# Which engine masks the diagonal blocks of the second batch, in decay attention followed by a max-MoE on one core

## The chip, the cores and the metric

The kernel runs on one core of one Trainium2 chip. The metric is the device time in microseconds (us) of one execution. The engines work side by side, each through its own instructions in order: TensorE (PE in the rows) multiplies matrices into PSUM, VectorE (DVE) and ScalarE (ACT) work element by element, GpSimd (POOL) reduces over partitions and casts, SyncE (SP) issues the transfers. An engine waits at the first instruction whose input is not there, and all that is queued behind it waits too.

## What is computed

```python
# q, k, v: 8 batches x 8 heads x 576 x 64; f: 8 x 8 x 576
scores = scale * q @ k.T + cum[:, None] - cum[None, :]    # cum: cumulated log of f
scores = where(key later than query, -1e9, scores)
attn = exp(scores - max) / (sum + 1e-9)
x = (attn @ v) laid out as 4608 tokens x 512
h = max(x @ w1, x @ w2, x @ w3)                            # 512 -> 768
out = h @ w_out                                            # 768 -> 512
```

Scores whose key is later than the query are masked. With keys on the partitions and queries along the row, this is a triangle in each 128 x 128 block on the diagonal, five per head (the fifth is 64 wide).

## The kernel before

**Heads.** The 64 heads are done one after another, eight to a batch. Each head is cut into unit 2, the first 256 queries (one PSUM bank, s2), and unit 1, the other 320 (three banks, s10 to s12). A unit's scores come in two passes on TensorE: pass A multiplies queries and keys (L647, two matmuls for unit 2, five for unit 1); then the diagonal blocks are masked; ScalarE and VectorE take the maximum over key blocks (L714, L702, L704, L707), GpSimd over the partitions (L717), and casts it into a row of the query tile (L720); pass B (L647 again) subtracts it by a further accumulation in the same bank. ScalarE takes the exponential (L735), VectorE or ScalarE and GpSimd sum it for the denominators where TensorE does not (L744 to L759).

**Masks.** Heads below MASKS are masked by TensorE, one small bf16 matmul of an identity with the mask per diagonal block (L663), accumulated in the bank between pass A and pass B. The others are masked by VectorE, which adds the mask to the bank in place: `cover` (L676, two blocks at a time; both units) and `cover_last` (L681, the 64 wide block; unit 1 alone).

**Pairs.** Two heads form a pair. TensorE multiplies the probabilities with the values (L803), and in the first two batches also sums them (L822). Of the sums, ScalarE takes a copy (L828); a transfer brings it into the tile sc, VectorE adds a small number and inverts (L898, L899), a second transfer writes to DRAM (rdram), a third reads it back widened (r_r), and VectorE multiplies the pair's values by it (L909). The result is one 128-row slice of x: ScalarE and VectorE split it into two parts (L914 xh, L916 xl).

**MoE.** For each batch, gemm1 (L940) runs over the four pairs of a batch and three matrices, three matmuls per pair and matrix (xh, xl, xh); gemm2 (L969) follows with three matmuls per block of 128 hidden columns. All weights are loaded, split (L511 to L523) and kept by then.

**Order.** All steps are handed to a planner (`Plan.add`) with engine, a cost and a due number, in units of a head. `Plan.emit` places, engine by engine, the due steps whose inputs it counts as there, and the kernel then issues them in that order. The constants that the change touches are offsets of these due numbers (WR and DPW for weights, LO, FO, VO1 and XO1 for the first two batches' sums, values and splits, lag for the MoE of the first batch), a preference for matmuls that follow one of like kind (LIKE), and the distance by which the load of a weight waits for an earlier one (PD).

Of the kernel before, what the change touches and what calls it, by code (L numbers as in the profile page):

```python
# [48 lines left out]
class Plan:  # L49
# [10 lines left out]
    ROOM = {"PE": (0.93, 0), "ACT": (1.0, -20.0), "DVE": (1.0, 0.0), "POOL": (1.0, 400.0), "SP": (1.0, 0)}  # L60
    LATE = 350.0
    MORE = (0.0, 100.0, 125.0, 0.0, 250.0)
    LIKE, HOLD = 4.0, 0.4

    def __init__(self):
        self.steps, self.wrote, self.read, self.parts = [], {}, {}, {}
# [1 line left out]
    def add(self, eng, cost, fn, r=(), w=(), prio=0.0, xfer=0.0, rows=128, short=0.0, light=False):  # L68
        i = len(self.steps)
        r, w = ([p for k in keys for p in self.parts.get(k, [k])] for keys in (r, w))  # L70
        deps = set()
        for k in r:
            if k in self.wrote:
                deps.add(self.wrote[k])
        for k in w:
            if k in self.wrote:
                deps.add(self.wrote[k])
            deps.update(self.read.pop(k, ()))
        for k in w:
            self.wrote[k] = i  # L80
        for k in r:
            if k not in w:
                self.read.setdefault(k, set()).add(i)
        deps.discard(i)
        self.steps.append((eng, cost, fn, deps, prio, xfer, rows, short, light))
# [86 lines left out]
def act_cost(cols):  # L172
    return 0.833 * cols + 60
# [7 lines left out]
def kernel(  # L181
# [33 lines left out]
    def sb(name, shape, dt=F32):  # L215
        return sbuf.tile(shape, dt, tag=name, name=name)
# [56 lines left out]
    NU = 5  # L273
    NB32 = 1

    MASKS, WIDE, COPIES = 16, 16, 64
    UT = [sb(f"u{i}", [P, S]) for i in range(KT)]

    XB = [sb(t, [P, 2, S2], F32R) for t in (f"u{KT}", "r")]
# [23 lines left out]
    def retire(old, new):  # L303
        gone = set()
        for key in [p for k in old for p in plan.parts.get(k, [k])]:
            gone |= plan.read.get(key, set()) | ({plan.wrote[key]} if key in plan.wrote else set())
        for key in [p for k in new for p in plan.parts.get(k, [k])]:
            plan.read.setdefault(key, set()).update(gone)
# [41 lines left out]
    def unit_w(i, fb):  # L350
        return lazy(f"w{3 * fb + i}", [P, 2, KT, P])

    def unit_o(fb):
        return lazy(f"w{3 * FT + fb}", [P, 2, DM])
# [12 lines left out]
    def dma(dst, src, r=(), w=(), prio=0.0, bytes_=300000):  # L367
        add("SP", 475 if bytes_ > 200000 else 640, lambda: nc.sync.dma_start(out=dst, in_=src), r, w, prio, bytes_ / 360)
# [118 lines left out]
    def load_weights(step, prio):  # L487

        if step < 3 * FT:
            i, fb = step % 3, step // 3  # L490
            src, n, m = (w1, w2, w3)[i].rearrange("(c p) f -> p c f", p=P), KT, P
            c0, c1 = fb * P, fb * P + P
            half = lambda t: unit_w(i, fb)[:, t]
        else:
            fb = step - 3 * FT
            src, n, m = w_out[fb * P:(fb + 1) * P, :].rearrange("(c p) e -> p c e", p=P), 1, DM
            c0, c1 = 0, DM
            half = lambda t: unit_o(fb)[:, t:t + 1]
        PD = 8
        raw, x = RAW[step], XW[step % len(XW)]  # L500
        key, kx, kh, kl = f"w{step}", f"x{step % len(XW)}", f"wh{step}", f"wl{step}"
        cols = lambda t: t.rearrange("p (c x) -> p c x", c=n)
        after = [f"wh{step - PD}"] if step >= PD else []
        if src.dtype == F32:
            dma(cols(raw.bitcast(F32)[:, 0:512]), src[:, :, c0:c1], w=[key], prio=DPW)
            add("DVE", 602, lambda: nc.vector.tensor_copy(x, raw[:, 0:512]), [key], [kx], prio)
        else:

            add("SP", 560, lambda: nc.sync.dma_start(out=cols(raw), in_=src.bitcast(I32)[:, :, 2 * c0:2 * c1]),  # L511
                after, [key], DPW + 0.01 * step, 524288 / 360)
            pair = raw.rearrange("p (x t) -> p x t", t=2)
            top, low = pair[:, :, 1], pair[:, :, 0]
            add("ACT", act_cost(512) + 40, lambda: nc.scalar.activation(
                top.bitcast(F32), top.bitcast(F32), AF.Prelu, scale=2.0 ** -112, alpha=2.0 ** 32), [key], [key], prio)
            add("DVE", 335, lambda: nc.vector.tensor_scalar(
                x, low, 29, None, op0=ALU.logical_shift_right), [key], [kx], prio)
            add("DVE", 602, lambda: nc.vector.scalar_tensor_tensor(
                x, top, 3, x, op0=ALU.logical_shift_left, op1=ALU.bitwise_or), [key, kx], [kx], prio)  # L520
        val = cols(x.bitcast(F32))
        add("ACT", act_cost(512) + 40, lambda: nc.scalar.activation(half(0), val, AF.Copy), [kx], [kh, key], prio)
        add("DVE", 602, lambda: nc.vector.tensor_tensor(half(1), val, half(0).bitcast(F32), op=ALU.subtract),  # L523
            [kx, kh], [kl], prio)
# [458 lines left out]
    def moe(b, prio):  # L983
        base = b * S
        if b % 2 == 0:
            chunks = [
                (0, S2, [main + (0, 0, S2)], [main + (0, 0), main + (128, 128)]),
                (S2, S1, [main + (0, 0, S2), midb + (S2, 0, 64)], [main + (0, S2), main + (128, S2 + 128)]),
            ]
        else:  # L990
            chunks = [
                (0, S1, [main + (64, 0, S2), midb + (0, 64, 64)],
                 [midb + (0, -64), main + (0, 64), main + (128, 192)]),
                (S1, S2, [main + (0, 0, S2)], [main + (0, S1), main + (128, S1 + 128)]),
            ]
        tot = sum(FT * 36 * mm_cost(c[1], P) + len(c[3]) * 18 * mm_cost(512, P) for c in chunks)
        done = 0.0
        for c0, cn, parts, outs in chunks:
            for fb in range(FT):
                gemm1(b, c0, cn, fb, parts, prio(done / tot))  # L1000
                done += 36 * mm_cost(cn, P)
            for hh, hl, kh, kl, col, row in outs:
                gemm2(hh, hl, kh, kl, col, base + row, prio(done / tot))
                done += 18 * mm_cost(512, P)


    LEAD, MLAG, WP, WR = 2.1, -0.1, 0.7, 0.65
    DP = -10.9
    DPW = 8.0
    ROWS = -4.0  # L1010
    warm_up()
    decay()
    QP = -0.3
    UO = 1
    LO = -2.55
    UP, VO, FO, XO = 0.4, 1.8, 0.5, -3.0
    HP, VP = -1.8, 0.6
    SP_ = 1.25
    HC, VO1, XO1, QP1, CB = -0.4, -1.2, -3.3, 0.7, -0.15
    order = (1, 2) if UO else (2, 1)  # L1020
    for n in range(H):
        load_raw(n, n - 8.9)
# [4 lines left out]
    for unit, up in ((2, 0.0), (1, 0.7)):  # L1027
        for n in range(H):
# [6 lines left out]
            if n % 4 == 3:  # L1035
                finish_group(n // 4, unit, p + LO)
    for n in range(H):
        retire([f"raw{n}/0", f"raw{n}/1"], [f"w{NW - H + n}"])
    for wstep in range(4 * FT):
        load_weights(wstep, WP + WR * wstep)  # L1040
# [11 lines left out]
    retire(["vn1"], [f"hdh{x}" for x in fbs])  # L1052
    for t in ("hmh", "hml"):
        retire([c + t for c in ("mx", "pf")] + [f"mx{t}a"], [f"{t}{x}" for x in fbs])
    lag = 0.15
    moe(0, lambda x: H + lag + H * x)
    retire([f"rs{g}{u}" for g in range(2) for u in (1, 2)], ["ph1"])
    retire([f"xa{x}" for x in range(KT)], ["pl1"])
# [63 lines left out]
```

## Time and profile before

| | |
|---|---|
| time, median of 3 runs | 905.31 us (905.06 to 907.84) |
| the profiled execution's own time | 907.01 us |
| its span in the trace | 905.2 us |
| mean granted clock of TensorE | 0.998 |
| TensorE busy, of the span | 895.2 us |
| VectorE, GpSimd, ScalarE busy | 630.1, 423.0, 387.8 us |
| matmul records in the trace | 6682 |

The profiled execution took 907.01 us, of which the span holds 905.2; 1.8 us lie around it. It is 1.7 us above the median. A busy TensorE means that matmuls were in its pipeline; how fast they follow one another is read from the distance of their starts, since their durations overlap.

### The profile page before, as it was taken

What the parts mean: (1) busy time and instruction counts of PE and PEld (TensorE: products, weight loads), DVE (VectorE), ACT (ScalarE), POOL (GpSimd) and SP (SyncE); (2) the same over time, 40 slices, a digit from 0 to 9 for tenths busy, and PEclk for the clock granted to TensorE, in tenths of its full rate; (3) what the DMA queues carried; (4) which work ended last, traced back from release to release, by engine and by line L of the source; (5) the groups of instructions that cost most, each with busy time, mean ns of one, the idle gap of its engine ahead of it and who ended that gap; (6) DMA issues with size and microseconds to landing.
All of it is one profiled execution on the core that took longest, in us unless ns stands there. A gap on an engine that the chain in (4) does not pass through costs nothing.

```text
span 905.2 us, 18386 instructions
## 1 busy us (share of the span) xinstructions
PE 895.2 (99%) x6682; PEld 809.6 (89%) x6682; DVE 630.1 (70%) x1427; ACT 387.8 (43%) x900; POOL 423.0 (47%) x380
## 2 busy tenths in 40 slices
PE   8999999999999999999999999999999999999998
PEld 6899988889989998988989898988989898998998
DVE  6989854577859796786858787796957678672211
ACT  6887633354334443443434443444334443342111
POOL 5443132336455645545555765556455464650000
PEclk9999999999999999999999999999999999999999
DMA  7995144555454456446445554546434454401000
GB/s 195 300 227 174 36 135 121 143 129 160 97 150 128 113 136 148 120 93 182 94 111 143 135 132 119 146 95 175 97 101 131 117 158 117 105 15 37 1 35 24
DMA packets 96867, 110.32 MB, mean 122 GB/s; under 512 B 51861, under 2 KB 64405, under 8 KB 96778
## 3 DMA queue, kind: packets, MB, share of 16 engines
q1 hardware_dynamic: 96778, 109.15, 46.4%
q8 instruction: 53, 0.87, 0.4%
q14 instruction: 36, 0.29, 0.1%
HBM read 49.56 MB, written 9.86 MB: 66 GB/s over the span
## 4 chain that ended last, share of the span: by engine, by line
PE 92%; DVE 3%; DMA 2%; ACT 1%; issue 1%; SPq 0%; ACTq 0%; DVEq 0%
PE mp L940 48%; PE mp L969 17%; PE s L647 13%; PE t L803 9%; PE t L772 1%; DMA w<-in_moe_w_dram 1%; DMA ks_r<-hl 1%; PE t L822 1%; PE mp L473 1%; DVE va_s L751 0%; DVE hl L536 0%; PE s L453 0%; PE mp L647 0%; PE s L663 0%; DVE hdl_r L954 0%
## 5 line engine op out<-in xcount | busy, mean ns | idle before, releaser
L940 PE MATMUL mp<-xh_r,w_r 128*128 128x320 f32 (+1 forms) x2160 | 462.3, 298 | 1.5 <-DVE tm L949 1.4
L940 PEld LDWEIGHTS mp<-xh_r,w_r 128*128 128x128 f32 x2160 | 355.8, 188 | 11.0 <-issue 4.7
L940 PE MATMUL mp<-xl_r,w_r 128*128 128x320 f32 (+1 forms) x1080 | 319.5, 296 | 0.0
L759 POOL PARTITION_ALL_REDUCE z<-va_s x96 | 193.8, 2018 | 160.6 <-DVE va_s L751 61.8
L717 POOL PARTITION_ALL_REDUCE gm<-mx x131 | 154.7, 1181 | 200.9 <-DVE mx L704 80.2
L940 PEld LDWEIGHTS mp<-xl_r,w_r 128*128 128x128 f32 x1080 | 203.3, 188 | 0.5
L949 DVE TENSOR_TENSOR tm<-mp,tm 128x256 f32<-128x256 f32 (+1 forms) x192 | 86.4, 450 | 86.0 <-PE mp L940 80.1
L647 PEld LDWEIGHTS s<-qs_r,ks_r 128*128 128x128 f32 (+1 forms) x784 | 116.2, 181 | 19.0 <-issue 14.0
L647 PE MATMUL s<-qs_r,ks_r 128*128 128x320 f32 (+4 forms) x784 | 132.2, 284 | 0.5 <-DMA ks_r<-hl 0.5
L969 PE MATMUL mp<-w_r,hmh_r 128*128 128x512 f32 (+1 forms) x396 | 122.7, 392 | 0.0
L707 DVE TENSOR_TENSOR mx<-mx,s 128x320 f32<-128x320 f32 (+3 forms) x248 | 92.2, 372 | 19.7 <-PE s L647 6.2
L969 PEld LDWEIGHTS mp<-w_r,hmh_r 128*128 128x128 f32 x396 | 70.1, 188 | 13.6 <-issue 1.8
L952 ACT ACTIVATE hmh_r<-tm 128x256 fp32r<-128x256 f32 x96 | 39.9, 416 | 96.4 <-DVE tm L949 95.8
L969 PE MATMUL mp<-w_r,hml_r 128*128 128x512 f32 (+1 forms) x198 | 76.9, 388 | 0.0
L947 ACT ACTIVATE tm<-mp 128x256 f32<-128x256 f32 (+1 forms) x96 | 39.6, 412 | 80.4 <-PE mp L940 76.0
L536 DVE STREAM_TRANSPOSE hl<-hl 128x576 f32<-128x576 f32 x56 | 68.4, 1242 | 4.8 <-DMA hl<-in_k_dram 4.8
L735 ACT ACTIVATE pf<-s 128x512 f32<-128x512 f32 (+4 forms) x107 | 49.0, 504 | 41.8 <-PE s L647 41.0
L954 DVE TENSOR_TENSOR hml_r<-tm,hmh_r 128x256 fp32r<-128x256 f32 x96 | 47.8, 498 | 17.6 <-ACT hmh_r L952 17.1
L720 POOL CAST qs_r<-gm 1x256 fp32r<-1x256 f32 (+1 forms) x112 | 56.4, 504 | 7.1
L676 DVE TENSOR_TENSOR s<-s,mask 128x256 f32<-128x256 f32 x96 | 40.6, 423 | 23.6 <-PE s L647 23.3
L735 ACT ACTIVATE ph_f<-s 128x384 f32<-128x384 f32 x80 | 36.0, 505 | 46.7 <-PE s L647 46.6
L714 ACT ACTIVATE mx<-s 128x320 f32<-128x320 f32 x56 | 24.4, 436 | 49.5 <-DVE s L681 42.1
(211 smaller groups left out, 1250.4 us busy)
## 6 DMA issues: line engine op xcount, KB each, us to landing
qs_r<-hl SPq DMA_DIRECT2D x168, 144.0 KB
ks_r<-hl SPq DMA_DIRECT2D x168, 144.0 KB
w<-in_moe_w_dram SPq DMA_DIRECT2D x18, 512.0 KB
out_dram<-o_r SPq DMA_DIRECT2D x35, 256.0 KB
hl<-in_q_dram SPq DMA_DIRECT2D x14, 576.0 KB
hl<-in_k_dram SPq DMA_DIRECT2D x14, 576.0 KB
r_r<-rdram SPq DMA_DIRECT2D x56, 144.0 KB
vn<-in_v_dram SPq DMA_DIRECT2D x30, 128.0 KB
```

Source lines behind the costliest of these rows:

```text
L536: add("DVE", 1085, lambda e=e, tt=tt, xs=xs: nc.vector.transpose(tt[:, e], xs[:, e]), [key + "0"], [key + "1"], prio)
L647: nc.tensor.matmul(bank[bk][0:l.shape[-1], col:col + w], l, rhs(qa, w), start=start and bk not in begun, stop=stop, skip_group_check=True)
L707: nc.vector.tensor_tensor(mt[:, a:a + w], mt[:, a:a + w], bank[bk][:, col:col + w], op=ALU.max)
L717: add("POOL", 450 + 2.6 * nq, lambda: nc.gpsimd.partition_all_reduce(gm, mt, P, bass.bass_isa.ReduceOp.max), [km, km + "a"], [kg], prio - CB)
L720: add("POOL", 130 + 0.9 * nq, lambda: nc.gpsimd.tensor_copy(QS(s)[96:97, 1, q0:q0 + nq], gm[96:97, :]), [kg], [kx], prio - CB)
L735: add("ACT", act_cost(w), lambda bk=bk, w=w, col=col: nc.scalar.activation(px()[:, col:col + w], bank[bk][:, 0:w], AF.Exp, scale=sc), [kb[ ...
L759: add("POOL", 520 + 5.1 * nq, lambda: nc.gpsimd.partition_all_reduce(Z[:, q0:q0 + nq], blocks_sum()[:, q0:q0 + nq], P, bass.bass_isa.Reduc ...
L803: nc.tensor.matmul(t[D * j:D * j + D, qa:qa + w], vn[:, j, c, 0:D], prs[j][0]()[:, col:col + w], start=x == 0, stop=True, skip_group_check ...
L940: nc.tensor.matmul(m, unit_w(i, fb)[:, w, kt, :], xx, start=kt == 0 and x == 0, stop=kt == KT - 1 and x == 2,)
L949: add("DVE", dve_cost(cn), lambda m=m: nc.vector.tensor_tensor(t, m, t, op=ALU.max), [km, kt_], [kt_], prio)
L954: add("DVE", dve_cost(w), lambda hh=hh, hl=hl, a=a, d=d, w=w: nc.vector.tensor_tensor(hl()[:, fb, d:d + w], t[:, a:a + w], hh()[:, fb, d:d ...
L969: nc.tensor.matmul(mp[:, 0:cn], l[:, fb, cs], unit_o(fb)[:, r, ds], start=fb == 0 and x == 0, stop=fb == FT - 1 and x == 2,)
```

## The change

MASKS goes from 16 to 8: the eight heads of the second batch (8 to 15) get L676 twice and L681 once on VectorE in place of five L663 matmuls on TensorE. Nine constants of the planner change with it.

```diff
-    LIKE, HOLD = 4.0, 0.4
+    LIKE, HOLD = 4.25, 0.4
...
-    MASKS, WIDE, COPIES = 16, 16, 64
+    MASKS, WIDE, COPIES = 8, 16, 64
...
-        PD = 8
+        PD = 7
...
-    LEAD, MLAG, WP, WR = 2.1, -0.1, 0.7, 0.65
+    LEAD, MLAG, WP, WR = 2.1, -0.1, 0.7, 0.8
     DP = -10.9
-    DPW = 8.0
+    DPW = 7.0
...
-    LO = -2.55
-    UP, VO, FO, XO = 0.4, 1.8, 0.5, -3.0
+    LO = -2.85
+    UP, VO, FO, XO = 0.4, 1.8, 1.0, -3.0
...
-    HC, VO1, XO1, QP1, CB = -0.4, -1.2, -3.3, 0.7, -0.15
+    HC, VO1, XO1, QP1, CB = -0.4, -0.95, -3.5, 0.7, -0.15
...
-    lag = 0.15
+    lag = 0.3
```

The order on TensorE is the same up to the first pass A of head 8 (66 us in the trace of before), and from some 225 us on nearly so: what differs there is a few exchanges between 706 and 816 us. Between 66 and 225 us the steps of the second batch and those of the first batch's MoE are interleaved anew, on all engines. There are three places that matter below.

**Place 1, TensorE, where the MoE of the second batch begins.** In the names, s10 to s12 are unit 1's banks, s2 is unit 2's, qs1/ks1 the odd heads' queries and keys, mp0 to mp2 gemm banks, w0 to w2 the first blocks of w1, w2, w3. Before, from the last matmul of pass A of head 17, unit 1:

```order
L647 MATMUL s12_127<-qs1_r_622,ks1_r_782 128x320
L969 MATMUL mp0_130<-w20_r_1246,hmh_r_953 128x512 x2
L969 MATMUL mp0_130<-w20_r_1246,hml_r_962 128x512
L969 MATMUL mp0_130<-w21_r_1294,hmh_r_953 128x512 x2
L969 MATMUL mp0_130<-w21_r_1294,hml_r_962 128x512
L969 MATMUL mp0_130<-w22_r_1310,hmh_r_953 128x512 x2
L969 MATMUL mp0_130<-w22_r_1310,hml_r_962 128x512
L969 MATMUL mp0_130<-w23_r_1363,hmh_r_953 128x512 x2
L969 MATMUL mp0_130<-w23_r_1363,hml_r_962 128x512
L647 MATMUL s2_128<-qs1_r_622,ks1_r_782 128x256
L647 MATMUL s2_128<-qs1_r_622,ks1_r_782 128x128
L940 MATMUL mp1_131<-xh_r_964,w0_r_505 128x320
```

After, from the same matmul:

```order
L647 MATMUL s12_127<-qs1_r_621,ks1_r_780 128x320
L940 MATMUL mp0_130<-xh_r_956,w2_r_594 128x320
L940 MATMUL mp0_130<-xl_r_1174,w2_r_594 128x320
L940 MATMUL mp0_130<-xh_r_956,w2_r_594 128x320
L647 MATMUL s2_128<-qs1_r_621,ks1_r_780 128x256
L647 MATMUL s2_128<-qs1_r_621,ks1_r_780 128x128
L940 MATMUL mp1_131<-xh_r_956,w0_r_504 128x320
L940 MATMUL mp1_131<-xl_r_1174,w0_r_504 128x320
L940 MATMUL mp1_131<-xh_r_956,w0_r_504 128x320
L940 MATMUL mp2_132<-xh_r_956,w1_r_532 128x320
L940 MATMUL mp2_132<-xl_r_1174,w1_r_532 128x320
L940 MATMUL mp2_132<-xh_r_956,w1_r_532 128x320
```

Before, the rest of the first batch's gemm2 stood behind this pass A, then pass B of unit 2, then 27 matmuls of gemm1 on the first three pairs, then pass A of head 18's unit 2 with pass B of head 17's unit 1, and only then gemm1 on the fourth pair (heads 14 and 15). After, gemm2 and most of those 27 stand ahead of it, and gemm1 on the fourth pair begins behind three matmuls and pass B of unit 2 (the row with w0). Pass B of head 17's unit 1 comes right behind the last row shown.

**VectorE at the same place.** u2 is the tile of the fourth pair. Before:

```order
L681 TENSOR_TENSOR s11_126<-s11_126,mask_64 128x64
L676 TENSOR_TENSOR s10_125<-s10_125,mask_64 128x2x128
L707 TENSOR_TENSOR mx1_82<-mx1_82,s12_127 128x320
L707 TENSOR_TENSOR mx1_82<-mx1_82,s10_125 128x320
L707 TENSOR_TENSOR mx1_82<-mx1_82,s10_125 128x192
L707 TENSOR_TENSOR mx1_82<-mx1_82,s11_126 128x64
L744 TENSOR_TENSOR va1_s_2276<-pl2_f_2355 128x128
L909 TENSOR_TENSOR u2_90<-u2_90,r_r_1675 128x576
L916 TENSOR_TENSOR xl_r_1187<-u2_90,xh_r_964 128x576
```

After:

```order
L681 TENSOR_TENSOR s11_126<-s11_126,mask_64 128x64
L676 TENSOR_TENSOR s10_125<-s10_125,mask_64 128x2x128
L707 TENSOR_TENSOR mx1_82<-mx1_82,s12_127 128x320
L707 TENSOR_TENSOR mx1_82<-mx1_82,s10_125 128x320
L707 TENSOR_TENSOR mx1_82<-mx1_82,s10_125 128x192
L707 TENSOR_TENSOR mx1_82<-mx1_82,s11_126 128x64
L909 TENSOR_TENSOR u2_90<-u2_90,r_r_1659 128x576
L744 TENSOR_TENSOR va1_s_2292<-pl2_f_2363 128x128
L916 TENSOR_TENSOR xl_r_1174<-u2_90,xh_r_956 128x576
```

L909 changes places with L744; both still stand behind the mask and the maximum of head 17's unit 1.

**Place 2, VectorE, the masks and maxima of head 15** (hl: later heads' queries and keys, transposed). Before, where TensorE masked:

```order
L536 STREAM_TRANSPOSE hl_73<-hl_73 128x18x32
L702 COPY mx2_83<-s2_128 128x128
L704 TENSOR_REDUCE mx2_83<-s2_128 128x128
L707 TENSOR_TENSOR mx1_82<-mx1_82,s12_127 128x320
L707 TENSOR_TENSOR mx1_82<-mx1_82,s10_125 128x320
L707 TENSOR_TENSOR mx1_82<-mx1_82,s10_125 128x192
L707 TENSOR_TENSOR mx1_82<-mx1_82,s11_126 128x64
```

After:

```order
L676 TENSOR_TENSOR s2_128<-s2_128,mask_64 128x2x128
L536 STREAM_TRANSPOSE hl_73<-hl_73 128x18x32
L702 COPY mx2_83<-s2_128 128x128
L704 TENSOR_REDUCE mx2_83<-s2_128 128x128
L681 TENSOR_TENSOR s11_126<-s11_126,mask_64 128x64
L676 TENSOR_TENSOR s10_125<-s10_125,mask_64 128x2x128
L536 STREAM_TRANSPOSE hl_73<-hl_73 128x18x32
L707 TENSOR_TENSOR mx1_82<-mx1_82,s12_127 128x320
L707 TENSOR_TENSOR mx1_82<-mx1_82,s10_125 128x320
L707 TENSOR_TENSOR mx1_82<-mx1_82,s10_125 128x192
L707 TENSOR_TENSOR mx1_82<-mx1_82,s11_126 128x64
```

Two transposes now lie within the head's own chain. On TensorE, the matmuls between pass A of head 15's unit 2 and pass B of its unit 1 are 18 of gemm1, 12 of gemm2, pass A of unit 1 and pass B of unit 2.

**Place 3, TensorE, the values of heads 14 and 15, unit 1** (pf1 and ph1 hold their probabilities). Before, they stand right behind pass B of head 15:

```order
L647 MATMUL s11_126<-qs1_r_622,ks1_r_782 64x64
L647 MATMUL s12_127<-qs1_r_622,ks1_r_782 128x320
L803 MATMUL t_129<-pf1_80,vl_77 64x64
L803 MATMUL t_129<-ph1_f_1447,vl_77 64x64
L803 MATMUL t_129<-pf1_80,vl_77 64x192
```

After, 12 matmuls of gemm1 stand between:

```order
L647 MATMUL s12_127<-qs1_r_621,ks1_r_780 128x320
L940 MATMUL mp0_130<-xh_r_956,w16_r_1126 128x320
L940 MATMUL mp0_130<-xl_r_1174,w16_r_1126 128x320
L940 MATMUL mp0_130<-xh_r_956,w16_r_1126 128x320 x2
L940 MATMUL mp0_130<-xl_r_1174,w16_r_1126 128x320
L940 MATMUL mp0_130<-xh_r_956,w16_r_1126 128x320 x2
L940 MATMUL mp0_130<-xl_r_1174,w16_r_1126 128x320
L940 MATMUL mp0_130<-xh_r_956,w16_r_1126 128x320 x2
L940 MATMUL mp0_130<-xl_r_1174,w16_r_1126 128x320
L940 MATMUL mp0_130<-xh_r_956,w16_r_1126 128x320
L803 MATMUL t_129<-pf1_80,vl_77 64x64
L803 MATMUL t_129<-ph1_f_1445,vl_77 64x64
```

## Rows read from the trace of the kernel before

**Rows 1.** Page: busy time of the engines, share of the span, instructions.

```profile
PE 895.2 (99%) x6682; PEld 809.6 (89%) x6682; DVE 630.1 (70%) x1427; ACT 387.8 (43%) x900; POOL 423.0 (47%) x380
```

**Rows 2.** Waits of TensorE: line, releaser, us in total, times, longest.

```profile
PE mp L473 <- DVE qs L481: 1.6, 1, 1.6
...
PE mp L940 <- DVE tm L949: 1.4, 1, 1.4
```

**Rows 3.** Timeline, TensorE, head 8's first pass A: start, us, instruction, idle before.

```profile
66.62 0.45 PE L647 MATMUL s<-qs_r,ks_r 128*128 128x256 f32 x2 [0.47 <-DMA ks_r<-hl]
```

**Rows 4.** Timeline, TensorE, values of heads 14 and 15.

```profile
183.71 0.33 PE L803 MATMUL t<-pf,vl 128*64 128x64 f32 x2
184.92 0.27 PE L803 MATMUL t<-ph_f,vl 128*64 128x64 f32 x1 [0.89 <-ACT ph_f L735]
```

**Rows 5.** Timeline, TensorE, head 15, pass A with masks, and a pass without.

```profile
175.40 0.32 PE L663 MATMUL s<-mask,ident 128*128 128x128 bf16 x3
175.56 0.42 PE L647 MATMUL s<-qs_r,ks_r 128*128 128x256 f32 x2
175.82 0.28 PE L663 MATMUL s<-mask,ident 128*128 128x128 bf16 x2
175.91 0.39 PE L647 MATMUL s<-qs_r,ks_r 128*128 128x320 f32 x1
...
181.87 0.34 PE L647 MATMUL s<-qs_r,ks_r 128*128 128x256 f32 x2
182.05 0.36 PE L940 MATMUL mp<-xh_r,w_r 128*128 128x320 f32 x1
```

**Rows 6.** Timeline, all engines, 191 to 208 us: head 17 and the fourth pair.

```profile
191.14 0.27 PE L822 MATMUL t<-pf,rx_r 128*32 128x128 f32 x1
...
201.21 0.80 PE L647 MATMUL s<-qs_r,ks_r 128*128 128x320 f32 x5
...
201.85 0.63 PE L969 MATMUL mp<-w_r,hmh_r 128*128 128x512 f32 x2
...
202.77 0.23 DVE L681 TENSOR_TENSOR s<-s,mask 128x64 f32<-128x64 f32 x1
...
203.56 1.65 DVE L707 TENSOR_TENSOR mx<-mx,s 128x320 f32<-128x320 f32 x4 [0.23 <-ACT mx L714]
...
205.30 1.24 POOL L717 PARTITION_ALL_REDUCE gm<-mx  x1
...
206.09 0.75 DVE L909 TENSOR_TENSOR u<-u,r_r 128x576 f32<-128x576 f32 x1
...
206.61 0.54 POOL L720 CAST qs_r<-gm 1x320 fp32r<-1x320 f32 x1
...
206.87 0.69 ACT L914 ACTIVATE xh_r<-u 128x576 fp32r<-128x576 f32 x1
...
207.59 0.76 DVE L916 TENSOR_TENSOR xl_r<-u,xh_r 128x576 fp32r<-128x576 f32 x1 [0.75 <-ACT xh_r L914]
```

**Rows 7.** Timeline, VectorE, unit 2 of head 18.

```profile
209.22 0.43 DVE L676 TENSOR_TENSOR s<-s,mask 128x256 f32<-128x256 f32 x1 [0.87 <-PE s L647]
...
209.96 0.41 DVE L704 TENSOR_REDUCE mx<-s 128x128 f32<-128x256 f32 x1
```

**Rows 8.** Chain of waits near the end: start, us, engine, line, instructions.

```profile
823.75 31.68 PE mp L940 x216
855.43 12.55 PE mp L969 x54
```

**Rows 9.** Groups by line, VectorE, 175 to 225 us: busy us, mean ns.

```profile
L536 DVE STREAM_TRANSPOSE hl<-hl 128x576 f32<-128x576 f32 x6 | 7.3, 1243 | 0.0
```

**Rows 10.** Stretches: us, busy per engine, then PEclk, DMA share, GB/s.

```profile
7.20:10.60 3.40, 1.85 (x20) 0.99 (x15) 2.85 (x5) 3.24 (x7) 2.98 (x5) 0.80 0.98 268
10.60:13.90 3.30, 3.30 (x40) 2.51 (x39) 0.45 (x1) 2.60 (x8) 0.00 (x0) 0.69 0.74 175
...
392.00:396.00 4.00, 2.65 (x19) 2.38 (x18) 3.38 (x7) 1.00 (x3) 2.55 (x2) 1.00 0.85 188
```

## Prediction, made before the changed kernel was run

> **What bounds the kernel now.** I read the page first. TensorE is busy in 895.2 of 905.2 us, VectorE in 630.1 [rows 1]. With so little idle, whatever takes issue time from TensorE shortens the kernel by that much, whatever makes it wait lengthens it, and nothing on another engine counts until TensorE waits for it. So the second view is TensorE's waits. They are seven and short; the longest are 1.6 us near the start and 1.4 us at 393 us [rows 2]; two more, of 0.5 and 0.9 us, lie in the stretch from 66 to 225 us that the change rearranges [rows 3, 4]. The third is the timeline of that stretch: what comes ready when, against how much TensorE work is placed in between. Outside that stretch the order hardly changes, and I put no term there.
>
> **Masks off TensorE.** 40 L663 matmuls and their weight loads go. In head 15 three masks stand between starts at 175.40 and 175.56, and two between 175.82 and 175.91: 0.16 + 0.09 = 0.25 us a head, 2.0 us for eight [rows 5]. The two matmuls between them took 0.26 us, against 0.18 us for such a pass without masks [rows 5]; if the masks' weight loads cause that too, it is 0.08 x 8 = 0.6 more. I take 2.0 as what the rows show directly; bounds 2.0 and 2.6.
>
> **Masks onto VectorE.** 16 of L676 at 0.43 us and 8 of L681 at 0.23 us are 8.7 us [rows 6, 7]. VectorE is idle for 275 us of the span [rows 1], so its time costs nothing by itself; it lengthens the way from pass A to pass B. That is hidden as long as the TensorE work placed between the two is longer than the way. In head 17, which VectorE masks already, the way of unit 1 is 207.15 - 202.01 = 5.1 us, from the end of pass A (201.21 + 0.80) to the end of the cast (206.61 + 0.54) [rows 6]. Counting the new order with 0.147 us for a gemm1 matmul (31.68 / 216) and 0.232 for one of gemm2 (12.55 / 54) [rows 8], 0.64 us for a pass of unit 1 [rows 6] and 0.18 for one of unit 2 [rows 5], unit 1 of heads 8 to 14 has at least 6.8 us of such work. Those masks I cost at nothing; where the cover is gone is told next.
>
> **Two waits that go.** Head 8's pass A waited 0.47 us for a transfer [rows 3]; it is now placed some 2.7 us of TensorE work later. Gain 0.5 (0 if the transfer moves with it, 0.6 at most). At 183.71 the values of heads 14 and 15 waited for the exponential: 1.21 us to the next start, of which some 0.1 is work [rows 4]. Twelve gemm1 matmuls (1.76 us) now stand ahead of them. Gain 1.0 (0.9 to 1.1); these twelve are work that had to be done anyway, so they cost nothing here.
>
> **A wait that comes: the fourth pair.** This is the largest term. In the new order TensorE goes from pass A of head 17's unit 1 through three gemm1 matmuls and a pass of unit 2 to gemm1 on the fourth pair: 0.64 + 0.44 + 0.18 = 1.26 us after that pass began [rows 5, 6, 8]. But VectorE's multiply for that pair, L909, is queued behind the mask and the maximum of this very pass. From the start of L681 the rows of before give 0.79 us to L707, 1.65 for L707, 0.78 from L909 to L914, 0.72 to L916 and 0.76 for it: xl is there 4.70 us after L681 began [rows 6]. L681 can begin when the pass has ended, 0.80 after its start, or as in the trace 1.56 after it, when VectorE had finished other sums [rows 6]. So xl comes 5.5 to 6.3 us after the pass began, against 1.26 + 0.15 (one matmul on xh first): TensorE idles 4.1 to 4.9 us. With before's whole distance, 208.35 - 201.21 = 7.14 us [rows 6], it is 5.7. I take 4.8. Behind the stopped matmul stand five more and pass B of head 17; its cast is done about 1.94 us after L707 [rows 6], 5.9 us after the pass began, so it adds nothing. Before, gemm2 and 27 gemm1 matmuls hid this way.
>
> The transfer of the sums says the same independently. From the last L822 at 191.14 to L909 took 14.95 us, to the end of L914 16.4 [rows 6]. In the new order 30 gemm1, 24 gemm2, three passes of unit 1 and four of unit 2 stand between: 4.4 + 5.6 + 1.9 + 0.7 = 12.6 us [rows 5, 6, 8], 3.8 us short. The two run side by side, so I count one. I see nothing late behind it: the next passes have 7 us and more of work in between.
>
> **A second, smaller one: head 15.** From pass A of unit 2 to pass B of unit 1 there are 18 x 0.147 + 12 x 0.232 + 0.64 + 2 x 0.18 = 6.4 us of work [rows 5, 6, 8]. VectorE needs: the pass 0.35 [rows 5], mask and maximum of unit 2 1.15 (209.22 to 210.37) [rows 7], a transpose of 1.24 [rows 9] in between, L681 to L707 0.79, another transpose, L707 1.65, then GpSimd 1.94 [rows 6]: 8.4 us. That leaves a wait of 1.9; I allow 0.2 for VectorE instructions that overlap and take 1.7 (1.2 to 2.0).
>
> **The clock.** TensorE's granted clock is 1.00 nearly everywhere. Behind the 1.6 us wait of L473 [rows 2] it was 0.80 over 3.4 us and 0.69 over the next 3.3 [rows 10], means of 2.4 GHz and 1.2 GHz: 0.68 + 1.02 = 1.7 us of TensorE time lost. Around the 1.4 us wait at 393 us it stayed at 1.00 [rows 2, 10]. A gap of 4.8 us is three times the one behind which it fell, so I count 1.7 (0, or 3.4 if it falls for both gaps).
> The Trainium skill ("TensorE: Matmul & The Clock Gate", Part 1) says that the halved clock is the default, that activity lifts it, and that an idle spell brings it back; the stretch behind L473 agrees (0.80 and 0.69), no row here shows a gap as long as the new one. By that rule the sum is the forecast below, 910.0; without a fall it would be 908.3. It speaks against this change.
>
> **Sum.** -2.0 - 0.5 - 1.0 + 4.8 + 1.7 + 1.7 = +4.7 us. Against the profiled execution's 907.01 us (span 905.2) that is 911.7; that run was 1.70 above the median, so against the median of 905.31 it is 910.0 us, 0.5% more. A measurement of this kernel tells about 0.3% (2.7 us) from no change: faster means under 902.6, slower over 908.0. With all bounds the other way the forecast's case runs from 908.1 (gains 4.2, waits 4.1 and 1.2, clock 1.7) to 911.9 (gains 2.9, waits 5.7 and 2.0, clock 1.7).
>
> **Rivals.**
> - *Idle, but the clock holds.* The same sum without the last term: 908.3 (906.4 to 910.2). For it: 1.4 us at 393 us left the clock at 1.00 [rows 10]. Against: 1.6 us did not. Half of it is within 0.3%, half slower.
> - *One of the two waits is hidden, or the large one is half as long.* VectorE may reach head 17's mask at once and transfers may land sooner than 14.95 us, since parts of that way were spent in queues that had no hurry: -3.5 + 2 to 4 us, without a fall of the clock, some 905.3. The rows speak against it in that 4.1 us of the large wait are durations of instructions.
> - *Gain alone; the other side.* If fewer than some 1.5 us of TensorE idle remain at L940 on the fourth pair, the change gives what the masks and the two waits are worth: 905.3 - 3.5 = 901.8 (901.1 to 902.4), faster. This needs TensorE to reach head 17's pass A with VectorE, GpSimd and the queues well ahead, and the split of the fourth pair ready. It decides at one place: whether L909 comes before TensorE does. For it speaks that all transitions to an MoE in before ran without a wait for xh or xl [rows 2]; against it that L909 stands behind this pass's own L707 on VectorE.
> - *VectorE falls behind.* The 8.7 us of masks show on TensorE in addition: up to 918. Against: heads 16 and later have the same masks and no wait for them [rows 2].
>
> **Chances.** Forecast (both waits and the fall) 0.45, all slower. Clock holds 0.20, half same and half slower. Half of the wait 0.12, same. Gain alone 0.20: 0.17 faster, 0.03 same. VectorE behind 0.03, slower. So faster 0.17, same 0.25, slower 0.58. The range runs from 902.8, which leaves the faster 0.17 out, to 912.2, which leaves out VectorE behind: 0.80. The likeliest case alone has 908.1 to 911.9.
>
> **What would show it.** TensorE's waits: a row of L940 waiting for L916 or L914 (xl_r, xh_r), once, 4 us or more, near 200 us; a row of L647 waiting for L720's qs_r, 1.2 to 2 us, some 25 us earlier; those of L803 on ph_f and L647 on ks_r gone. 48 L663 matmuls, 112 L676, 56 L681. A stretch of PEclk under 1.00 right behind the long wait. The forecast is wrong if no L940 waits for more than 1.5 us near 200 us, or if the clock stays at 1.00 behind it, or if the masks prove worth more than 2.6 us.

## The result, and the profile after

The changed kernel takes 910.05 us in the median of 5 runs (909.35 to 910.85), the kernel before 905.83 in the runs beside it (905.06 to 907.84): a ratio of 1.0046, with an interval of 1.0035 to 1.0057. It is 4.2 us slower; 4.7 were forecast.

The page of the changed kernel (busy time, share, instructions) has the same TensorE time in a longer span (908.1 us, 905.2 before):

```profile
PE 895.3 (99%) x6642; PEld 809.0 (89%) x6642; DVE 634.6 (70%) x1451; ACT 387.7 (43%) x900; POOL 424.1 (47%) x380
```

40 matmuls are gone (6,682 to 6,642), as [rows 1] against this row shows, yet TensorE counts as busy for as long as before: part of its work ran at half the clock. (The trace of before has a fall of the clock near its start [rows 10]; this one has 1.00 there.) Its waits between 60 and 240 us (line, releaser, us in total, times, longest):

```profile
PE mp L940 <- ACT xh_r L914: 3.6, 1, 3.6
PE mp L969 <- ACT tm L947: 1.1, 2, 0.6
PE mp L940 <- DVE xl_r L916: 0.2, 1, 0.2
```

The waits of [rows 3] and [rows 4] are not among them. The new one is where it was expected. The timeline of all engines around it (start, us, instruction, idle before), to be read beside [rows 6]:

```profile
192.00 0.27 PE L822 MATMUL t<-pf,rx_r 128*32 128x128 f32 x1
...
203.82 0.81 PE L647 MATMUL s<-qs_r,ks_r 128*128 128x320 f32 x5
...
204.90 0.34 PE L647 MATMUL s<-qs_r,ks_r 128*128 128x256 f32 x2
204.93 0.23 DVE L681 TENSOR_TENSOR s<-s,mask 128x64 f32<-128x64 f32 x1
...
205.72 1.65 DVE L707 TENSOR_TENSOR mx<-mx,s 128x320 f32<-128x320 f32 x4 [0.23 <-ACT mx L714]
...
207.29 0.76 DVE L909 TENSOR_TENSOR u<-u,r_r 128x576 f32<-128x576 f32 x1
...
208.08 0.69 ACT L914 ACTIVATE xh_r<-u 128x576 fp32r<-128x576 f32 x1 [1.61 <-DVE u L909]
...
208.80 0.76 DVE L916 TENSOR_TENSOR xl_r<-u,xh_r 128x576 fp32r<-128x576 f32 x1
```

```profile
208.82 0.64 PE L940 MATMUL mp<-xh_r,w_r 128*128 128x320 f32 x1 [3.58 <-ACT xh_r L914]
209.61 0.63 PE L940 MATMUL mp<-xl_r,w_r 128*128 128x320 f32 x1 [0.16 <-DVE xl_r L916]
```

TensorE runs out of work at 204.90 + 0.18 = 205.08 and goes on at 208.82: 3.74 us, and some 0.5 to 0.6 more until xl. Behind it lies the clock (stretch: us, busy per engine, then PEclk, DMA share, GB/s):

```profile
204.90:208.70 3.80, 0.34 (x4) 0.19 (x2) 3.46 (x9) 1.75 (x4) 3.39 (x2) 0.99 0.76 236
208.70:215.50 6.80, 6.53 (x29) 6.06 (x31) 3.84 (x9) 2.38 (x7) 3.96 (x4) 0.50 0.47 108
215.50:222.00 6.50, 6.50 (x53) 5.34 (x51) 4.46 (x12) 1.65 (x4) 4.25 (x4) 1.00 0.86 263
```

The granted clock falls to 0.50 (1.2 GHz) as the gap ends and stays there for 6.8 us. That is twice the stretch which [rows 10] suggested.

### The profile page after: what moved, and what is told of

The parts are those of the page before. It is cut to its first block, busy times and chain, and to the rows that moved or that the text cites. A ratio compares the mean times of both kernels' runs of the same rounds, so it can differ in the third digit from the quotient of the medians.

```text
span 908.1 us, 18341 instructions
## 1 busy us (share of the span) xinstructions
PE 895.3 (99%) x6642; PEld 809.0 (89%) x6642; DVE 634.6 (70%) x1451; ACT 387.7 (43%) x900; POOL 424.1 (47%) x380
## 4 chain that ended last, share of the span: by engine, by line
PE 93%; ACT 2%; DVE 2%; SPq 1%; issue 1%; DMA 1%; ACTq 0%; DVEq 0%
PE mp L940 51%; PE mp L969 17%; PE s L647 13%; PE t L803 9%; PE t L772 2%; PE t L822 1%; DMA hl<-in_q_dram 1%; SPq L368 0%; ACT w L515 0%; PE mp L772 0%; DVE va_s L751 0%; PE t L858 0%; SPq L440 0%; ACT hl L540 0%; ACT ph_f L735 0%
## 5 line engine op out<-in xcount | busy, mean ns | idle before, releaser
L940 PE MATMUL mp<-xh_r,w_r 128*128 128x320 f32 (+1 forms) x2160 | 465.4, 299 | 4.9 <-ACT xh_r L914 3.6
L940 PEld LDWEIGHTS mp<-xh_r,w_r 128*128 128x128 f32 x2160 | 357.2, 189 | 14.6 <-issue 5.8
L940 PE MATMUL mp<-xl_r,w_r 128*128 128x320 f32 (+1 forms) x1080 | 320.3, 297 | 0.2 <-DVE xl_r L916 0.2
L940 PEld LDWEIGHTS mp<-xl_r,w_r 128*128 128x128 f32 x1080 | 203.8, 189 | 1.1 <-DVE xl_r L916 0.5
L949 DVE TENSOR_TENSOR tm<-mp,tm 128x256 f32<-128x256 f32 (+1 forms) x192 | 86.4, 450 | 77.4 <-PE mp L940 72.8
L647 PEld LDWEIGHTS s<-qs_r,ks_r 128*128 128x128 f32 (+1 forms) x784 | 117.4, 182 | 18.2 <-issue 13.9
L647 PE MATMUL s<-qs_r,ks_r 128*128 128x320 f32 (+4 forms) x784 | 131.9, 285 | 0.0
L969 PE MATMUL mp<-w_r,hmh_r 128*128 128x512 f32 (+1 forms) x396 | 123.0, 392 | 1.1 <-ACT tm L947 1.1
L707 DVE TENSOR_TENSOR mx<-mx,s 128x320 f32<-128x320 f32 (+3 forms) x248 | 92.2, 372 | 23.0 <-PE s L647 12.5
L969 PEld LDWEIGHTS mp<-w_r,hmh_r 128*128 128x128 f32 x396 | 70.0, 188 | 15.1 <-issue 1.8
L969 PE MATMUL mp<-w_r,hml_r 128*128 128x512 f32 (+1 forms) x198 | 76.9, 388 | 0.0
L676 DVE TENSOR_TENSOR s<-s,mask 128x256 f32<-128x256 f32 x112 | 47.6, 425 | 40.5 <-PE s L647 40.2
L536 DVE STREAM_TRANSPOSE hl<-hl 128x576 f32<-128x576 f32 x56 | 68.9, 1243 | 4.8 <-DMA hl<-in_k_dram 3.7
L947 ACT ACTIVATE tm<-mp 128x256 f32<-128x256 f32 (+1 forms) x96 | 39.6, 412 | 76.0 <-PE mp L940 71.7
L720 POOL CAST qs_r<-gm 1x256 fp32r<-1x256 f32 (+1 forms) x112 | 55.7, 498 | 7.2
```

Source lines behind the costliest of these rows:

```text
L536: add("DVE", 1085, lambda e=e, tt=tt, xs=xs: nc.vector.transpose(tt[:, e], xs[:, e]), [key + "0"], [key + "1"], prio)
L647: nc.tensor.matmul(bank[bk][0:l.shape[-1], col:col + w], l, rhs(qa, w), start=start and bk not in begun, stop=stop, skip_group_check=True)
L707: nc.vector.tensor_tensor(mt[:, a:a + w], mt[:, a:a + w], bank[bk][:, col:col + w], op=ALU.max)
L720: add("POOL", 130 + 0.9 * nq, lambda: nc.gpsimd.tensor_copy(QS(s)[96:97, 1, q0:q0 + nq], gm[96:97, :]), [kg], [kx], prio - CB)
L940: nc.tensor.matmul(m, unit_w(i, fb)[:, w, kt, :], xx, start=kt == 0 and x == 0, stop=kt == KT - 1 and x == 2,)
L949: add("DVE", dve_cost(cn), lambda m=m: nc.vector.tensor_tensor(t, m, t, op=ALU.max), [km, kt_], [kt_], prio)
```

## Experiments: what made the gap

The prediction read the gap off the new order. It did not say why the order came out so. My theory: a head masked by VectorE has a longer way from pass A to pass B, the second batch's heads fall behind the first batch's MoE, and by the time of heads 14 and 15 too little MoE work is left to cover the transfers and splits of the fourth pair. The rivals: the planner's new constants; or the TensorE work itself, which is missing as cover once 40 matmuls are gone. Four runs on one chip tell them apart; the kernel before took 906.16 us beside them.

**Masks alone** (MASKS 8, every other constant as before):

```diff
-    MASKS, WIDE, COPIES = 16, 16, 64
+    MASKS, WIDE, COPIES = 8, 16, 64
```

> MASKS is 8, all nine constants are those of before. If the masks' move alone makes the new order (theory), the counted TensorE work from the last L822 of heads 14 and 15 to gemm1 on the fourth pair is 12.9 us as in the changed kernel: one wait of L940 for L914 of 3 to 4.5 us near 205 us, the granted clock at 0.50 behind it, 909 to 911 us. If the constants are to blame (rival), no such wait and 902 to 903 us.

910.36 us, ratio 1.0046 (1.0032 to 1.0061), with the same wait. The clock falls behind it, but for a shorter time: a mean of 0.75 over the 6.8 us of the last row is 3.4 us at 0.50, half of what the changed kernel's trace has behind the same gap.

```profile
209.43 0.41 PE L940 MATMUL mp<-xh_r,w_r 128*128 128x320 f32 x1 [3.58 <-ACT xh_r L914]
210.22 0.55 PE L940 MATMUL mp<-xl_r,w_r 128*128 128x320 f32 x1 [0.39 <-DVE xl_r L916]
```

```profile
209.20:216.00 6.80, 6.19 (x38) 5.35 (x40) 3.89 (x11) 2.83 (x8) 4.33 (x5) 0.75 0.49 107
```

**Constants alone** (the other way round):

```diff
-    MASKS, WIDE, COPIES = 8, 16, 64
+    MASKS, WIDE, COPIES = 16, 16, 64
```

> MASKS is 16, the nine constants are the new ones. Theory (constants hardly matter): the counted work to the fourth pair is 18.3 us as before, no wait of L940 for L914, within 1 us of before. Rival (constants to blame): the wait is there with 16 masks too, 909 us or more.

906.86 us, 1.0009 (0.9999 to 1.0018), and no wait of L940 for L914. The nine constants are cleared: the move of the masks alone makes the wait and the time.

**Both engines mask** heads 8 to 15:

```diff
-    MASKS, WIDE, COPIES = 8, 16, 64
+    MASKS, WIDE, COPIES = 16, 16, 64
...
-        if not mask_pe:
+        if n >= H:
             add("DVE", 335, cover, ["const"], [kb[0]], prio)
```

> The changed kernel's constants; heads 8 to 15 are masked by TensorE and then once more by VectorE, so TensorE keeps its 40 matmuls and the heads' way gets VectorE's masks. Theory (the longer way of a head makes the second batch late against the first MoE): the wait at the fourth pair stays, 3 us or more, and the masks' 2.0 us are lost: 911 to 914 us. Rival (the TensorE work taken out is what is missing as cover): no wait of L940 over 1 us, within 1.5 us of before.

912.39 us, 1.0072 (1.0056 to 1.0089). TensorE has all its work back and still stops, now for head 17's cast and then for xl:

```profile
209.97 0.45 PE L647 MATMUL s<-qs_r,ks_r 128*128 128x256 f32 x2 [3.19 <-POOL qs_r L720]
...
211.39 0.64 PE L940 MATMUL mp<-xl_r,w_r 128*128 128x320 f32 x1 [0.55 <-DVE xl_r L916]
```

**No engine masks** heads 8 to 15 (the outputs of that batch lack the mask):

```diff
-        mask_pe = n < MASKS
+        mask_pe = n < 2 * H
...
-                if mask_pe and bk in banks:
+                if n < MASKS and bk in banks:
...
```

> The changed kernel's constants; the diagonal blocks of heads 8 to 15 are masked by no engine, so TensorE loses the 40 matmuls and VectorE gets nothing (the outputs of the second batch lack the mask). Theory (the longer way): no wait at the fourth pair, 2 to 3.5 us below before, 902.3 to 903.8. Rival (missing cover): the wait stays, 907 us or more.

902.12 us, 0.9957 (0.9942 to 0.9972), just below the expected range, and no wait for the fourth pair. So it is not the missing TensorE work: without it, and without VectorE's masks, the time falls by 4.0 us, where the gains of the prediction add up to 3.5. It is the masks on VectorE. Where the heads lose the time shows in unit 1 of head 11, of which pass A and pass B are these rows of TensorE's timeline, first in the changed kernel, then without masks, then with both:

```profile
129.55 0.79 PE L647 MATMUL s<-qs_r,ks_r 128*128 128x320 f32 x5
...
142.88 0.81 PE L647 MATMUL s<-qs_r,ks_r 128*128 128x320 f32 x5
```

```profile
127.12 1.02 PE L647 MATMUL s<-qs_r,ks_r 128*128 128x256 f32 x7
...
136.18 0.81 PE L647 MATMUL s<-qs_r,ks_r 128*128 128x320 f32 x5
```

```profile
130.09 0.58 PE L647 MATMUL s<-qs_r,ks_r 128*128 128x320 f32 x4
...
144.27 0.88 PE L647 MATMUL s<-qs_r,ks_r 128*128 128x320 f32 x5
```

From start to start it is 13.3 us, about 9.0, and 14.2. Over unit 1 of all eight heads of the batch (from the 64 wide matmul of pass A to that of pass B) the traces give 59.5 us in the kernel before and with the constants alone, 58.8 without masks, but 69.9 in the changed kernel and with the masks alone, and 69.1 with both; head 11 has about half of the difference. The masks themselves are 0.6 us a head; the rest is what the planner puts around them. VectorE's timeline in the changed kernel:

```profile
132.87 1.19 DVE L536 STREAM_TRANSPOSE hl<-hl 128x576 f32<-128x576 f32 x1
133.91 0.27 DVE L681 TENSOR_TENSOR s<-s,mask 128x64 f32<-128x64 f32 x1
134.10 0.36 DVE L676 TENSOR_TENSOR s<-s,mask 128x256 f32<-128x256 f32 x1
136.25 1.36 DVE L542 SCALAR_TENSOR_TENSOR hl<-hl 128x1152 fp32r<-128x1152 f32 x1 [1.79 <-ACT hl L540]
137.53 1.65 DVE L707 TENSOR_TENSOR mx<-mx,s 128x320 f32<-128x320 f32 x4
```

Pass A was done at 130.34. The mask begins at 133.91, behind transposes and splits of the next four heads' inputs, and the maximum at 137.53, behind an L542 that waited 1.79 us for ScalarE. An instruction more on VectorE in a head's way is one more place where the queue lets something else in. That this interleaving, not the masks' own 0.6 us, is the larger part is read from these rows and sums; no run took it away by itself.

**Masks on VectorE for the last two heads only**, the kernel before otherwise:

```diff
-    MASKS, WIDE, COPIES = 16, 16, 64
+    MASKS, WIDE, COPIES = 14, 16, 64
```

> The kernel before with MASKS 14: VectorE masks heads 14 and 15 alone. The counted cover is 16.9 us from the last L822 to the fourth pair and 9.6 us from pass A of head 17. Theory (a few lengthened heads leave enough cover): no wait of L940 for L914 over 0.5 us, ten matmuls less, within 1.5 us of before (904.5 to 906.5). Rival (any head masked by VectorE in this batch opens the gap): 3 us of waiting, 908 or more.

913.08 us, 1.0081 (1.0068 to 1.0094). The wait for the fourth pair is gone as expected, but the time is 7 us off: it lies where the rival put it, without the wait by which the rival explained it. TensorE stops at head 15's own pass B:

```profile
183.57 1.48 PE L647 MATMUL s<-qs_r,ks_r 128*128 128x320 f32 x5 [2.90 <-POOL qs_r L720]
```

and later batches, whose order changed too, wait more than before (L940 for L949 2.3 us in four places). So counting TensorE's cover at one place does not price an order. What ran beside GpSimd's cast is in the last section.

## Experiments: the clock

**Matmuls that fill the gap**, into the bank of the values, which nothing uses then:

```diff
+                    if b == 1 and c0 == 0 and fb == 0 and i == 0 and kt == 3:
+                        z = ident.rearrange("p (o x) -> p o x", o=1).broadcast_to((P, 4, P))
+                        for _ in range(17):
+                            nc.tensor.matmul(TPS.rearrange("p (o x) -> p o x", o=4), ident, z, start=True, stop=True)
                     for x, (w, xx) in enumerate(((0, hh), (0, ll), (1, hh))):
```

> The changed kernel with 17 further matmuls of 512 columns (identity by identity, into the bank of the values, which nothing reads then) on TensorE right before gemm1 on the fourth pair, some 3.7 us that fill the gap and compute nothing that is used. If the long gap is what lowers the clock (theory): the granted clock stays at 1.00 from 205 to 216 us, the wait of L940 for L914 is under 0.5 us, and the kernel is 3 to 3.4 us faster than the changed one, 906.5 to 907. If the clock falls for another reason (rival), the time is that of the changed kernel, 909.5 to 910.5.

908.88 us, 1.0030 (1.0014 to 1.0045) of before. Timeline and stretch of this kernel:

```profile
204.92 3.85 PE L942 MATMUL t<-ident 128*128 128x512 bf16 x17
208.66 0.41 PE L944 MATMUL mp<-xh_r,w_r 128*128 128x320 f32 x1
209.45 0.41 PE L944 MATMUL mp<-xl_r,w_r 128*128 128x320 f32 x1 [0.38 <-DVE xl_r L916]
```

```profile
209.00:216.00 7.00, 6.62 (x50) 5.33 (x50) 5.22 (x13) 3.08 (x8) 4.47 (x4) 1.00 0.58 134
```

The gap is filled, gemm1 begins at the same time (208.66 to 208.82), and the clock stays at 1.00: it is the idle stretch that lowers it. By the starts of the same matmuls in the two traces, this kernel is 0.15 us ahead at the gap and 2.6 at 216 us: the fall of 6.8 us costs 2.5 us at its place. Against the trace with the masks alone, whose fall lasts 3.4 us, its lead grows from 0.8 to 2.2 us: 1.4 us. But the median is only 1.2 us below the changed kernel's, where 3 to 3.4 were expected, and those times are of another session, so both were run side by side:

> The changed kernel as it is, to stand beside the next run on the same chip: 909.3 to 911, one wait of 3.6 us of L940 for L914 and the granted clock at 0.50 for 6 to 7 us behind it.

> The changed kernel with the 17 filling matmuls, on the same chip as the run before. From the two traces the fall of the clock costs 2.5 us at the place where it happens; if that is kept to the end, this is 1.8 to 2.6 us faster than the run before. If the gain is lost on the way (rival), under 1 us.

909.80 (909.64 to 910.20) for the changed kernel, 909.26 for the filled one in ten runs (908.65 to 915.20), whose ratio to before is 1.0050 (1.0033 to 1.0067): 0.5 us less, where 1.8 to 2.6 were expected. Runs that spread so far settle no half microsecond. Six of the ten kept a mean granted clock of 1.00; their median is 908.76, 1.0 us below the changed kernel's, while the two of 914.87 and 915.20 have 0.994. In the traces the filled kernel is 2.5 us ahead of its partner over the fall of the clock (from 0.34 behind to 2.14 ahead), and 0.9 ahead from 400 us on; it has small waits that the changed kernel does not have:

```profile
PE s L647 <- DMA qs_r<-hl: 0.4, 1, 0.4
...
PE mp L944 <- ACT o_r L980: 0.3, 1, 0.3
```

The lead drops at just these two: from 2.14 to 1.52 us where pass A waits for the transfer (242.60 us), and from 1.42 to 0.86 where gemm1 waits for ScalarE to empty a bank (314.21 us). A kernel that comes there earlier meets inputs that are not ready. The first pair of traces shows that this need not be so much: of 2.6 us there, 2.0 are left at the end.

So the price of the fall is settled where it happens, 2.5 us for the long one and 1.4 for the short one. Of the 2.5 us, 1.9 are left at the end of the traces in one pair, 1.3 in the other; the medians say some 1 us.

## Experiments: can the gap be closed

**Inputs of heads 16 to 19 prepared earlier** (their transfers, L536, L540, L542 due one head earlier), then of all such groups:

```diff
-            load_quad(b, h // 4, p - (QP1 if b < 2 else QP))
+            load_quad(b, h // 4, p - (QP1 if b < 2 else QP) - (1.0 if n == 16 else 0.0))
```

```diff
-            load_quad(b, h // 4, p - (QP1 if b < 2 else QP))
+            load_quad(b, h // 4, p - (QP1 if b < 2 else QP) - (1.0 if n >= 12 else 0.0))
```

> The changed kernel with the load of the third batch's first four heads (16 to 19: the transfers, transposes L536 and splits L540, L542) due one head earlier. In its order the counted work from the last L822 of heads 14 and 15 to the fourth pair is 16.1 us instead of 12.9, and from pass A of head 17 to it 12.7 instead of 1.3. Theory: the wait of 3.6 us and the fall of the clock go, at most 0.5 us of waiting left there: 902 to 903.5 us. Rival (the masks on VectorE cost elsewhere too): 905 us or more without the wait.

> As the run before, with every such load of four heads from head 12 on due one head earlier. The same cover (16.1 and 11.0 us), and no unit with less than 6.2 us (unit 1) or 4.4 us (unit 2) of TensorE work between its passes. Theory: 902 to 903.5 us, at most 0.5 us below the run before. If the loads come too early for their buffers, transfers wait and it is slower than that run.

915.12 (1.0097, 1.0079 to 1.0115) and 920.62 us (1.0164, 1.0149 to 1.0179): 11.6 and 17 us above the theory's range. By its time the first falls to the rival (905 or more without the wait at the fourth pair), and the second is slower than the first, though no row has a transfer as the reason. The first has no wait at the fourth pair, as counted, but this one instead; the stretch above it shows VectorE busy in 6.87 of 7 us:

```profile
178.00:185.00 7.00, 4.53 (x23) 3.38 (x21) 6.87 (x11) 3.48 (x5) 1.46 (x2) 1.00 0.14 30
```

```profile
186.66 0.41 PE L940 MATMUL mp<-xh_r,w_r 128*128 128x320 f32 x1 [3.54 <-DVE tm L949]
```

L949, which frees gemm1's banks, stood behind two L542 and the maximum L707. The second run waits in many places for L949 and L947, 7.9 us in all.

**Heads 8 to 15 due one head later:**

```diff
-        p = n - LEAD
+        p = n - LEAD + (1.0 if n < 16 else 0.0)
```

> The changed kernel with heads 8 to 15 due one head later. In its order VectorE's multiply L909 for the fourth pair stands ahead of the next head's mask, and 11.7 us of TensorE work lie between pass A of head 17 and gemm1 on that pair (1.3 in the changed kernel), but only 13.5 us from the last L822 of heads 14 and 15, where the transfers and the split need 16.4 us. If the way of the sums alone is long enough to stop TensorE: a wait of L940 for L914 of 2 to 3.5 us, a fall of the clock, 907.5 to 910. If only VectorE's order does it: no wait over 1 us there, 902 to 904.

919.27 us, 1.0143 (1.0128 to 1.0158), outside both expectations: 3.5 us for L949 as above, 3.7 us of L803 for L830, and only 1.0 for L916 at the most. Too much else moved; whether the sums' way alone would have stopped TensorE stays open.

**The casts of heads 8 to 17 on ScalarE:**

```diff
-            add("POOL", 130 + 0.9 * nq, lambda: nc.gpsimd.tensor_copy(
+            add("ACT" if n < 18 else "POOL", act_cost(nq) if n < 18 else 130 + 0.9 * nq, lambda: nc.scalar.activation(QS(s)[96:97, 1, q0:q0 + nq], gm[96:97, :], AF.Copy) if n < 18 else nc.gpsimd.tensor_copy(
```

> The changed kernel with the casts of heads 8 to 17 (L720) on ScalarE in place of GpSimd, which shortens each head's way from pass A to pass B by some tenths and takes it out of GpSimd's queue and out of the stretches in which VectorE's L542, L909 or L916 hold a cast of GpSimd up. In its order the cover is 14.4 us from the last L822 and 4.1 from pass A of head 17, where the changed kernel has 12.9 and 1.3. Theory: a wait of L940 for L914 or L916 of 1 to 2.5 us in place of 4.4, the clock keeps 1.00 if the gap is under 1.6 us and may fall above it: 904.5 to 908. Rival (the length of the heads' way doesn't set the gap): 909 to 911.

908.85 us, 1.0037 (1.0024 to 1.0049), a little above the theory's range, and not clear of the changed kernel's 1.0046 (1.0035 to 1.0057). The 3.74 us gap becomes two smaller waits near 205 and 208 us, and the clock falls behind them all the same (0.53 from 210 to 215 us):

```profile
205.37 0.41 PE L940 MATMUL mp<-xh_r,w_r 128*128 128x320 f32 x1 [1.07 <-ACT o_r L976]
...
208.73 1.54 PE L647 MATMUL s<-qs_r,ks_r 128*128 128x320 f32 x5 [1.77 <-ACT qs_r L720]
```

A shorter way narrows the gap, which fits the theory; that it makes the kernel faster is not shown. No version with the masks of this batch on VectorE beat the kernel before.

## Why the prediction was right, point by point

- **Masks, 2.0 us.** As forecast. In the trace of before, the 40 L663 of heads 8 to 15 take 2.0 us in all, from the start of each to the next start on TensorE (2.2 with the constants alone). The kernels without masks and with the constants alone, side by side, agree roughly: 906.86 - 902.12 = 4.7 us, of which TensorE's waits between 60 and 240 us are 2.4 - 0.4 = 2.0 in the profiled executions. That leaves 2.7, over the bound of 2.6, but with waits of single executions.
- **The two waits that go, 1.5 us.** Both went. Not foreseen: two waits of L969 for L947, 0.47 us at 112.97 and 0.59 at 179.71, where gemm2 follows at once in a bank that gemm1 has just filled and ScalarE must empty first.
- **The fourth pair, 4.8 us.** 3.74 + 0.5 to 0.6 = 4.3, inside 4.1 to 5.7. Term by term the way stood as [rows 6] gave it: L681 to L707 0.79, L909 to L914 0.79, L914 to L916 0.72. L681 came 1.11 us after the pass began, between the bounds of 0.80 and 1.56. The second count held as well: from the last L822 to the end of L914 16.8 us, 16.4 predicted. This mechanism was right, though the row has 3.58 and 0.16 us where the sign named 4 or more.
- **Head 15, 1.7 us.** This mechanism was wrong. The row that was named as its sign, L647 waiting for L720's qs_r, is not there: pass B of unit 1 waited some 0.2 us. VectorE and GpSimd needed 7.5 us for what was counted as 8.4, since successive instructions overlap by more than the 0.2 allowed, and TensorE reached pass B later, held 0.75 us by L947 at 179.71. With the other wait of L969 (at 112.97, about 0.5) these make 1.4 to 1.5: near the number by luck, for another reason.
- **The clock, 1.7 us.** It fell. By the Trainium skill ("TensorE: Matmul & The Clock Gate", Part 1) an idle spell brings the halved clock back; the trace agrees, with 0.50. The size was off for this execution: 6.8 us long and 2.5 us dear, where [rows 10] showed a stretch half as long; with the masks alone the same gap brought 3.4 us, for 1.4. Nor is a wait of 1.6 us a sure sign, as the term took it from [rows 2]: the last section has waits of that length without a fall.
- **Sum.** -2.0 - 0.5 - 1.0 + 4.3 + 1.4 + 2.5 = +4.7. By the starts of the same matmuls in the traces of before and after, the changed kernel loses 5.0 us between 64 and 220 us and makes up 0.9 of it behind; 4.1 remain, and the medians say 4.2. The prediction had neither the longer fall nor that part of the loss is given back. That they nearly cancel, and that the waits of L969 stand in for head 15, is luck; that the fourth pair costs more than all the gains bring is not.
- Three slips change nothing: the second longest wait of before, 1.5 us at the start of the span (L453), was passed over; the gains at their most add up to 4.3, not 4.2; and the top of the forecast's case is 911.8, not 911.9.
- What the prediction lacked is the cause. It took the order as given; the runs show that the order follows from the masks on VectorE. That it does so by way of the heads' pace is read from the ways of the eight heads and from the run with the casts on ScalarE. Its sentence that VectorE's masks are "hidden" held for TensorE's waits at each head, but they took the cover from the next batch's start.

## What to carry to other kernels

Work taken off the bounding engine and put onto the way of a dependent chain can be lost twice: the chain falls behind the filler work that covered it, and the gap opens later, where the filler is used up. Count, at each hand-over, the work placed between the producer and the consumer against the measured way, on every engine in order; and add the price of the clock to any gap of some microseconds on TensorE (1.4 to 2.5 us here, part of it given back later). But a count at one place tells of that place alone: three of the orders above that were well covered there were slower elsewhere.

## What the runs showed of the hardware

**A gap can lower the clock for longer than it lasts.** In all traces of this case, single waits of TensorE of 2.25, 2.90, 3.19 and (masks alone) 3.58 us were followed by 3.4 us at 0.50; waits of 3.54, 3.58 and 3.67 us by 6.8 us; two waits of 1.07 and 1.77 us within 5 us by 6.8 us too. Among the shorter single ones it went both ways: 1.55 us (before [rows 2], masks alone) and 1.66 us (heads due later) were followed by 3.4 us at 0.50, but these two, the first with the constants alone, the second in the filled kernel, were not, and their executions have a granted clock of 1.000; nor was one of 1.93 us with the inputs of heads 16 to 19 earlier:

```profile
PE s L647 <- DMA qs_r<-hl: 1.6, 1, 1.6
```

```profile
PE mp L473 <- DVE qs L481: 1.8, 1, 1.8
```

Nor was the wait of 1.4 us near 393 us [rows 2]. So the length of a gap alone did not decide it; what else does, no run here shows.

**GpSimd's cast takes longer beside some of VectorE's instructions.** L720, a cast of one row, takes 448 ns in the median but up to 3,035. With masks on heads 14 and 15 alone, VectorE's and GpSimd's timelines read:

```profile
180.59 2.60 DVE L542 SCALAR_TENSOR_TENSOR hl<-hl 128x1152 fp32r<-128x1152 f32 x2
183.12 1.07 DVE L949 TENSOR_TENSOR tm<-mp,tm 128x320 f32<-128x320 f32 x2
```

```profile
180.48 3.04 POOL L720 CAST qs_r<-gm 1x320 fp32r<-1x320 f32 x1
```

The cast ended 0.3 us after the two L542, and TensorE's 2.90 us wait is this. In the kernel before, 9 of 112 casts took over 0.9 us, and each of them overlapped L542, L909 or L916 on VectorE, which read two tensors from SBUF; 23 casts that ran beside L536 or L707 alone, which read at most one from SBUF, took 394 to 451 ns. The longest of the nine is this one:

```profile
507.58 2.02 DVE L916 TENSOR_TENSOR xl_r<-u,xh_r 128x576 fp32r<-128x576 f32 x3
```

```profile
507.86 2.06 POOL L720 CAST qs_r<-gm 1x320 fp32r<-1x320 f32 x1
```

That the overlap is the cause is read from these coincidences; no run took L542 away from a cast.
